# One visit to the quarters of the array: the block-diagonal product together with the next pair's k^T v and q^T

## The chip, the cores and the metric

The kernel runs on one core of one Trainium2 chip. Its time is the device time in microseconds (us) of one execution. Three executions of the kernel before took 942.20, 940.97 and 944.48 us, so the median is 942.2 us. The profiled execution has a span of 942.4 us and a granted TensorE clock of 1.000 throughout.

The engines are named as in the profile: PE is TensorE (matmuls; PEld its weight loads), DVE is VectorE, ACT is ScalarE, POOL is GpSimd and SP is SyncE, whose queue issues most of the transfers.

## The reference

There are two stages. The first is linear attention, on q, k and v of shape (8 batches, 8 heads, 576 rows, 64):

```
kv  = einsum('bhsd,bhse->bhde', k, v)
out = einsum('bhsd,bhde->bhse', q, kv)
rms = sqrt(mean(out * out, axis=-1) + 1e-06)
attn = out / rms * g_norm
```

Each head thus needs k^T v (64x64, a sum over 576 rows), the product of q with it, and a normalisation over the 64 columns of every row. The heads are laid side by side to x of 4608 x 512, and the second stage is a feed-forward block with w_in (512 x 2048) and w_out (2048 x 512):

```
h = x @ w_in
sp = maximum(h, 0) + log1p(exp(-abs(h)))
g = h * erf(sp)
return g @ w_out
```

## The kernel before

**Groups, pairs and tiles.** The rows are worked in nine groups T. Groups 0 to 7 are the first 512 rows (G) of each batch; group 8 is made of the 64 last rows (R) of all eight batches. A group's attention is done two heads at a time: four pairs p to a group (NP). A group's hidden layer is 16 tiles of 128 columns (FC), taken in four batches of four (BATCH), and then four projections j of 128 rows each.

**Three numbers for one.** From group 2 on (FIRST) the feed-forward matmuls don't use plain fp32. Each operand is cut into three fp32r forms, and `product` (L522) makes 12 matmuls of 128x512 for one 128x512 result: eight into n_ps and four into m_ps. `upper` (L478, ScalarE), `lower_only` (L481) and `both_only` (L484, VectorE) cut the forms: x_forms of the group's input and g_forms of the hidden layer. The weights' forms are written to DRAM in groups 0 and 1 and streamed back for each later group.

**The main loop** (L866) goes over rounds m, one for each batch b of each group. A round has four hidden tiles of the current batch, then the four projections of the batch before, and, in between, one pair of the *next* group's attention. So the attention of groups 3 to 7 is done in 20 rounds, while groups 2 to 6 go through their feed-forward block. In each round:

- hidden tile i: `product` on TensorE, then a scaled copy of n_ps on ScalarE (L916), an add of m_ps on VectorE (`add`, L518), and softplus on ScalarE (L931). In the first two tiles the g_forms of the batch before are cut as well (L478 twice on ScalarE, L481 and L484 twice on VectorE);
- after the fourth tile: erf over the batch (L935), behind a load of its function table;
- projection j: `result` (L840): `product`, then two VectorE operations into e (L513 or L851, and L518);
- after the second projection: the gating product h * s (L958).

**The pair's attention** is a list of pieces that `attention` (L282) returns, and `places` (L881) says where in the round each of them is put: (0, 2, 3, 5, 6, 8), where place 1 to 4 are after hidden tiles 1 to 4, and 5 to 8 after projections 1 to 4. In the last round of a group the sixth place is 7. The pieces for groups 1 to 7 are:

- `products` (L310), place 0, before the first hidden tile: k^T v for the two heads (ten matmuls of 115 or 116 rows and 64 columns, L326), and q^T by four 128x128 transposes (L353). For even pairs q_last, the last 64 rows of two pairs, is transposed as well (L334). VectorE copies k^T v to bd_kv (L340, then L342 twice, the two copies that swap partition halves), and the tail of q^T (L348); ScalarE copies q^T to qT (L354).
- `apply_quad` (L356), place 2: the block-diagonal product. The array is used as four quarters of 64x64; four matmuls of 256 columns (L362), and two for the tail (L370). The result stands in at_ps, a tile of two PSUM banks. ScalarE squares it (L374).
- `keep_tail` and `halve`, place 3: VectorE keeps the tail's result in x_last (L377) and cuts the square into two fp32r parts (L397, L398). `loads` then asks for the pair two rounds ahead.
- `mean`, place 5: four matmuls (L413, L414) that average over a head's columns, into the upper half of at_ps; then Ln, Exp and Square on ScalarE (L428, L429, L430), between two table loads.
- `norm`, place 6: three VectorE operations (L436, L439, L448), the last giving x.
- `split`, place 8: x to x_forms (L478, L481, L484).

**What sets the order.** The schedule is written by hand (`manual_schedule`): each engine runs its instructions in the order in which the program emits them. Within a round a piece's instructions therefore stand on ScalarE and VectorE behind those of the hidden tile just before its place, and ahead of those of the next. [...]two belong to at_ps, and six are handed out as three pairs by turns to `product` (the list `banks`, L520). A pair of banks comes free when the copy or add of both results is done.

**The layout of q.** For groups 1 to 7 each partition of q_sb holds four consecutive rows of q, and two of the four row blocks are loaded with the two heads swapped, by four transfers (L134 to L136). So the transposed q stands where the quarters want it. `store` (L600) writes the results back to rows in steps of four.

Of the kernel before, what the change touches and what calls it, by code (L numbers as in the profile page):

```python
# [39 lines left out]
FP32 = mybir.dt.float32  # L40
# [3 lines left out]
AF = mybir.ActivationFunctionType  # L44
# [10 lines left out]
FIRST = 2  # L55
# [5 lines left out]
def kernel(  # L61
# [56 lines left out]
    def chunks(T):  # L118

        return 6 if T == 0 else 5  # L120

    def load_pair(i):
        T, p = divmod(i, NP)
        if T >= B:
            return
        pool = early if i in (2, 3) else kvp
        side = nc.scalar if i < 3 else nc.sync
        t = q_sb[T, p] = pool.tile([P, J, 2, D], FP32, name="q_sb", tag="q")
        rows = q[T, 2 * p : 2 * p + 2, 0:G, :].rearrange("h (p j) d -> p j h d", j=J)
        if T == 0:  # L130
            nc.sync.dma_start(out=t, in_=rows)
        else:

            for i in range(2):  # L134
                for js, to in ((slice(0, J // 2), i), (slice(J // 2, J), 1 - i)):
                    nc.sync.dma_start(out=t[:, js, to], in_=rows[:, js, i])  # L136
        for name, got, src in (("k", k_sb, k), ("v", v_sb, v)):
            C = chunks(T)
            rows, rest = divmod(S, C)
            assert rest < 2  # L140
            t = got[T, p] = pool.tile([rows + rest, 2, C, D], FP32, name=f"{name}_sb", tag=name)
            heads = src[T, 2 * p : 2 * p + 2]
            side.dma_start(
                out=t[:rows].rearrange("r h c d -> r h (c d)"),
                in_=heads[:, : S - rest].rearrange("h (r c) d -> r h (c d)", c=C),
            )
            if rest:
                side.dma_start(
                    out=t[rows:, :, 0], in_=heads[:, S - rest :].rearrange("h r d -> r h d")
                )  # L150
# [125 lines left out]
    def at_pool(bufs):  # L276
# [2 lines left out]
        ps_now[:] = [at_room.enter_context(tc.tile_pool(name="ps_at", bufs=bufs, space=PSUM))]  # L279
        return ps_now[0]  # L280

    def attention(T, p, pools=None):  # L282

        st = {}

        halves = FIRST <= T < B
        quad = 0 < T < B
        side = (slice(0, D), slice(D, 2 * D))

        def two(t):  # L290
            return t.rearrange("p (a t) -> p a t", a=2) if quad else t
        bd = bd_kv[:, (T * NP + p) % 2, :]

        q_tail, o_tail = slice(P, 2 * P), slice(2 * P, 2 * P + R)

# [8 lines left out]
        def square_tile(name):  # L304

            if T == 0:
                return gate.tile([P, G], FP32, name=name, tag="h")
            return attp.tile([P, G], FP32, name=name, tag="qT")

        def products():  # L310

            if quad:

                pool = at_pool(2)
                kv_ps, qt_ps = (
                    pool.tile([P, G], FP32, name=name, tag="at") for name in ("kv_ps", "qt_ps")
                )
            else:
                kv_ps = st["kv"] = bank("kv_ps")
            ks, vs, qs = (x.pop((T, p)) for x in (k_sb, v_sb, q_sb))  # L320
            C = chunks(T)
            for c in range(C):
                rows = slice(0, S // C + (c < S % C))
                for i in range(2):
                    s = slice(i * D, i * D + D)
                    nc.tensor.matmul(  # L326
                        kv_ps[s, 0:D] if quad else kv_ps[s, s],
                        lhsT=ks[rows, i, c],
                        rhs=vs[rows, i, c],
                        start=(c == 0),  # L330
                        stop=(c == C - 1),
                    )
            if p % 2 == 0:
                nc.tensor.transpose(kv_ps[:, q_tail], q_last[:, p // 2], ident)  # L334
            if p == NP - 2:
                for i in range(NP):
                    load_last(T + 1, i)
            st["qT"] = square_tile("qT")
            if quad:
                nc.vector.tensor_copy(out=bd[:, 0:D], in_=kv_ps[:, 0:D])  # L340
                for i in range(2):
                    nc.vector.tensor_copy(out=bd[side[1 - i], D : 2 * D], in_=kv_ps[side[i], 0:D])  # L342
            else:
                for s in side:
                    nc.vector.tensor_copy(out=bd[s, s], in_=kv_ps[s, s])
            if p % 2 == 0:
                tails[T] = attp.tile([P, P], FP32, name="qT_last", tag="t")
                nc.vector.tensor_copy(out=tails[T], in_=kv_ps[:, q_tail])  # L348
            st["tail"] = tails[T][:, p % 2 * R : p % 2 * R + R]
            if not quad:  # L350
                qt_ps = bank("qt_ps")
            for j in range(J):
                nc.tensor.transpose(qt_ps[:, j * P : j * P + P], qs[:, j], ident)  # L353
            nc.scalar.copy(st["qT"], qt_ps)  # L354

        def apply_quad():  # L356

            qT, tail = st["qT"], st.pop("tail")
            at = st["at"] = at_pool(1).tile([P, 2, G], FP32, name="at_ps", tag="at")
            x = two(qT)  # L360
            for a, i, o in ((0, 0, 0), (0, 1, 1), (1, 0, 1), (1, 1, 0)):
                nc.tensor.matmul(  # L362
                    at[side[o], a, 0 : 2 * P],
                    lhsT=bd[side[i], a * D : a * D + D],
                    rhs=x[side[i], a],
                    start=True,
                    stop=True,
                )
            for s in side:
                nc.tensor.matmul(  # L370
                    at[s, 0, 2 * P : 2 * P + R], lhsT=bd[s, 0:D], rhs=tail[s], start=True, stop=True
                )
            st["o"] = at[:, :, 0 : 2 * P]
            nc.scalar.activation(x, st["o"], AF.Square)  # L374

        def keep_tail():
            nc.vector.tensor_copy(  # L377
                out=x_last[:, p, T * R : T * R + R], in_=st["at"][:, 0, 2 * P : 2 * P + R]
            )

        def apply():
            qT, o_ps, kv_ps = st["qT"], bank("se_ps"), st.pop("kv")
            nc.tensor.matmul(kv_ps[:, o_tail], lhsT=bd, rhs=st.pop("tail"), start=True, stop=True)
            nc.tensor.matmul(o_ps, lhsT=bd, rhs=qT, start=True, stop=True)
            nc.vector.tensor_copy(out=x_last[:, p, T * R : T * R + R], in_=kv_ps[:, o_tail])
            st["o"] = o_ps
            nc.scalar.activation(qT, o_ps, AF.Square)

        def square():
            st["o"], st["qT"] = x_last[:, p, :], square_tile("sq")  # L390
            nc.scalar.activation(st["qT"], st["o"], AF.Square)

        def halve():
            sq = st.pop("qT")
            hi = st["hi"] = attp.tile([P, G], FP32R, name="sq_hi", tag="rms_r")
            lo = st["lo"] = attp.tile([P, G], FP32R, name="sq_lo", tag="sq_lo")
            nc.vector.tensor_copy(out=hi, in_=sq)  # L397
            nc.vector.tensor_tensor(out=lo, in0=sq, in1=hi.bitcast(FP32), op=ALU.subtract)  # L398

        def mean(table=True):  # L400
# [13 lines left out]
                    nc.tensor.matmul(ps, lhsT=mean_w, rhs=lo[:, a], start=False, stop=True)  # L414
                u = square_tile("u")
            else:
                u = st.pop("qT")
                for ps, a in parts:
                    nc.tensor.matmul(
                        ps, lhsT=mean_w.bitcast(FP32), rhs=two(u)[:, a], start=True, stop=True  # L420
# [38 lines left out]
                thirds(st.pop("x"), *(form[:, p] for form in x_forms[T]))  # L459

        def loads():
            load_pair(T * NP + p + 2)

        if T == 0:
            return products, apply, halve, mean, norm
        if T == B:
            return lambda: None, square, lambda: None, mean, norm, split

        if halves:
            pieces = ((products,), (apply_quad,), (keep_tail, halve, loads))  # L470
        else:
            pieces = ((products, loads), (apply_quad,), (keep_tail,))
        return (*(partial(chain, *group) for group in pieces), mean, norm, split)


# [43 lines left out]

    banks = [(ps_h, "h"), (ps_h, "h")] + [(ps_o, f"o{i}") for i in range(4)]  # L520

    def product(weights, moving, turns=True, cuts=1):  # L522


        n_ps, m_ps = (
            pool.tile([P, G], FP32, name=name, tag=tag)
            for name, (pool, tag) in zip(("n_ps", "m_ps"), banks[:2])
        )
        if turns:
            banks.extend(banks[:2])  # L530
            del banks[:2]
        spans = [slice(i * G // cuts, (i + 1) * G // cuts) for i in range(cuts)]
        for ps, forms, cols in [(n_ps, (0, 1), slice(0, G))] + [(m_ps, (2,), x) for x in spans]:
            for k in range(4):
# [64 lines left out]

    def store(T, j, e, cols=slice(0, DM)):  # L600
        if T < B:
            rows = out[T * S : T * S + G, :].rearrange("(p j) f -> p j f", j=J)
            nc.sync.dma_start(out=rows[:, j, :], in_=e)
            return
        for h, side in enumerate((nc.sync, nc.scalar)):
            first_row = (2 * j + h) * S + G
            side.dma_start(
                out=out[first_row : first_row + R, cols], in_=e[h * R : h * R + R, cols]
            )
# [388 lines left out]
```

## Time and profile before

| | share or time |
|---|---|
| span of the profiled execution | 942.4 us |
| TensorE busy | 923.0 us, 98% |
| VectorE busy | 721.1 us, 77% |
| ScalarE busy | 617.3 us, 66% |
| chain that ended last: TensorE, VectorE, ScalarE | 48%, 22%, 19% |
| mean DMA rate | 276 GB/s |
| k^T v, L326: 656 records | 27.8 us, 235 ns each |
| q^T, L353: 128 records | 21.0 us, 289 ns each |
| block-diagonal product, L362: 224 records | 18.6 us, 402 ns each |
| its tail, L370: 112 records | 7.9 us, 217 ns each |
| k^T v to bd_kv, L340 and L342 | 6.1 us and 12.4 us |
| q^T to SBUF, L354 | 18.7 us |

One plain fp32 matmul shows as two records in the trace. Matmuls overlap in the array, so the mean duration of a record is longer than the time from one start to the next, and the latter is what counts in a stream. "Busy" of a matmul engine in a dense stream is near 100% whatever it does. Durations of VectorE and ScalarE instructions are also somewhat longer than the distance between the starts of two that follow each other (the 128x512 copy L916 takes 0.59 us, and the next can start 0.47 us after a PSUM read of that size began).

The rounds of groups 3 to 7's attention lie between about 254 and 748 us; the rows below in the prediction are from there.

### The profile page before, as it was taken

How to read it: one execution, taken by the hardware profiler on the slowest of the kernel's cores; microseconds unless marked ns; L12 is line 12 of the kernel's file. 1: busy time of each engine (PE TensorE's matmuls, PEld its weight loads, DVE VectorE, ACT ScalarE, POOL GpSimd, SP SyncE). 2: the span in 40 equal slices, each digit the busy share in tenths (PEclk: the TensorE clock that was granted, in tenths of full speed). 3: DMA queues.
4: the chain of work that ended last, by engine and by line, in shares of the span. 5: the costliest groups of instructions: out<-in, count | busy, mean ns of one | idle time of the engine just before them, and what ended most of it. 6: DMA issues, size and time to landing. Idle time of an engine off the chain costs nothing.

```text
span 942.4 us, 12548 instructions
## 1 busy us (share of the span) xinstructions
PE 923.0 (98%) x4556; PEld 683.0 (72%) x4556; DVE 721.1 (77%) x1046; ACT 617.3 (66%) x825; POOL 2.4 (0%) x10
## 2 busy tenths in 40 slices
PE   5899999999999999999999999999999999999998
PEld 4444445566588888888888888888888788888886
DVE  2857648888578888888888888888888877788667
ACT  3899776778666666666666666666666666665552
POOL 1000000000000000000000000000000000000000
PEclk9999999999999999999999999999999999999999
DMA  9776405888699888898889889988896779777972
GB/s 252 253 213 213 145 19 197 328 337 338 209 360 352 316 311 282 301 330 290 275 297 328 293 280 328 319 297 287 290 337 250 265 251 355 274 279 290 354 272 60
DMA packets 109605, 259.83 MB, mean 276 GB/s; under 512 B 45336, under 2 KB 68200, under 8 KB 109544
## 3 DMA queue, kind: packets, MB, share of 16 engines
q1 hardware_dynamic: 107832, 256.74, 77.4%
q10 hardware_dynamic: 1648, 2.29, 0.9%
q8 instruction: 36, 0.59, 0.2%
q14 instruction: 25, 0.20, 0.1%
q0 software_dynamic: 64, 0.00, 0.0%
HBM read 224.40 MB, written 34.60 MB: 275 GB/s over the span
## 4 chain that ended last, share of the span: by engine, by line
PE 48%; DVE 22%; ACT 19%; issue 6%; DMA 4%; SPq 1%; DVEq 0%; ACTq 0%
PE n_ps L536 21%; PE m_ps L536 10%; PE o_ps L592 9%; DVE h L518 5%; PE h_ps L766 4%; DVE g_forms L481 4%; ACT s L935 4%; DVE e L518 2%; ACT L105 2%; ACT s L931 2%; ACT L935 2%; ACT h L916 2%; DMA q_sb<-in_q_dram 2%; DVE e L513 2%; DVE x L448 1%
## 5 line engine op out<-in xcount | busy, mean ns | idle before, releaser
L536 PE MATMUL n_ps<-w_out_parts,g_forms 128*128 128x512 f32 x928 | 232.0, 392 | 0.0
L536 PE MATMUL n_ps<-x_forms,w_in_parts 128*128 128x512 f32 x896 | 226.8, 395 | 0.3 <-DVE x_forms L481 0.3
L536 PEld LDWEIGHTS n_ps<-w_out_parts,g_forms 128*128 128x128 f32 x928 | 172.8, 188 | 37.1 <-issue 1.4
L931 ACT ACTIVATE s<-h 128x512 f32<-128x512 f32 x112 | 70.9, 633 | 184.7 <-DVE h L518 184.7
L536 PEld LDWEIGHTS n_ps<-x_forms,w_in_parts 128*128 128x128 f32 x896 | 165.2, 188 | 35.1 <-DVE x_forms L481 0.8
L518 DVE TENSOR_TENSOR h<-m_ps,h 128x512 f32<-128x512 f32 x116 | 79.8, 688 | 59.5 <-ACT h L916 44.8
L536 PE MATMUL m_ps<-w_out_parts,g_forms 128*128 128x512 f32 (+1 forms) x468 | 124.2, 388 | 0.0
L536 PE MATMUL m_ps<-x_forms,w_in_parts 128*128 128x512 f32 x448 | 120.1, 390 | 0.0
L592 PE MATMUL o_ps<-w_out_sb,h_sb 128*128 128x512 f32 x224 | 101.5, 596 | 0.2 <-DVE h_sb L716 0.2
L536 PEld LDWEIGHTS m_ps<-w_out_parts,g_forms 128*128 128x128 f32 x468 | 87.5, 188 | 18.5
L536 PEld LDWEIGHTS m_ps<-x_forms,w_in_parts 128*128 128x128 f32 x448 | 84.1, 188 | 18.1
L518 DVE TENSOR_TENSOR e<-m_ps,e 128x512 f32<-128x512 f32 (+1 forms) x117 | 80.3, 687 | 18.3 <-PE m_ps L536 11.5
L513 DVE SCALAR_TENSOR_TENSOR e<-n_ps,e 128x512 f32<-128x512 f32 x88 | 60.3, 686 | 33.4 <-PE n_ps L536 32.3
L592 PEld LDWEIGHTS o_ps<-w_out_sb,h_sb 128*128 128x128 f32 x224 | 41.4, 190 | 44.4 <-issue 41.9
L484 DVE SCALAR_TENSOR_TENSOR g_forms<-g_forms 128x1024 fp32r<-128x1024 f32 x58 | 71.1, 1225 | 2.0
L481 DVE TENSOR_TENSOR g_forms<-h,g_forms 128x1024 fp32r<-128x1024 f32 x58 | 70.4, 1215 | 1.2 <-ACT g_forms L478 1.2
L766 PE MATMUL h_ps<-xT,w_in_sb 128*128 128x512 f32 x144 | 64.6, 594 | 3.4 <-DVE w_in_sb L245 1.9
L916 ACT ACTIVATE h<-n_ps 128x512 f32<-128x512 f32 x112 | 65.6, 586 | 3.1 <-PE n_ps L536 3.0
L478 ACT ACTIVATE g_forms<-h 128x1024 fp32r<-128x1024 f32 x58 | 58.9, 1058 | 12.2 <-PE m_ps L536 8.7
L958 DVE TENSOR_TENSOR h<-h,s 128x1024 f32<-128x1024 f32 x56 | 66.0, 1219 | 0.7 <-ACT s L935 0.7
L108 ACT ACT_TABLE_LOAD x44 | 56.5, 1283 | 0.7
L935 ACT ACTIVATE s<-s 128x1024 f32<-128x1024 f32 x56 | 56.2, 1052 | 0.3
(108 smaller groups left out, 990.8 us busy)
## 6 DMA issues: line engine op xcount, KB each, us to landing
w_out_parts<-w_out SPq DMA_DIRECT2D x116, 768.0 KB
w_in_parts<-w_in SPq DMA_DIRECT2D x112, 768.0 KB
w_in<-w_new SPq DMA_DIRECT2D x16, 768.0 KB
w_raw<-in_moe_w_in_dram SPq DMA_DIRECT2D x16, 512.0 KB
w_raw<-in_moe_w_out_dram SPq DMA_DIRECT2D x8, 1024.0 KB
out_dram<-e SPq DMA_DIRECT2D x32, 256.0 KB
k_sb<-in_k_dram SPq DMA_DIRECT2D x28, 287.5 KB
v_sb<-in_v_dram SPq DMA_DIRECT2D x28, 287.5 KB
```

Of the source, the lines that this page charges most:

```text
L478: nc.scalar.activation(high, x, AF.Copy, scale=1.0 + 2.0**-13)
L481: nc.vector.tensor_tensor(out=low, in0=x, in1=high.bitcast(FP32), op=ALU.subtract)
L484: nc.vector.scalar_tensor_tensor(out=both, in0=low.bitcast(FP32), scalar=SHIFT, in1=high.bitcast(FP32), op0=ALU.mult, op1=ALU.add,)
L513: nc.vector.scalar_tensor_tensor(out=out_, in0=ps, scalar=scale, in1=out_, op0=ALU.mult, op1=ALU.add)
L518: nc.vector.tensor_tensor(out=out_, in0=ps, in1=out_, op=ALU.add)
L536: nc.tensor.matmul(ps[:, cols], lhsT=weights(form, k), rhs=moving(form, k)[:, cols], start=(form == forms[0] and k == 0), stop=(form == fo ...
L592: nc.tensor.matmul(o_ps[j], lhsT=g[:, j * P : j * P + P], rhs=w_out_sb[:, f, :], start=(f == 0), stop=last,)
L766: nc.tensor.matmul(plain[i], lhsT=w_in_sb[:, i % FC, c], rhs=xT[T][:, c, :], start=(c == 0), stop=(c == KC - 1),)
L916: nc.scalar.activation(h[:, i], n_ps, AF.Copy, scale=SHIFT - 1.0)
L931: nc.scalar.activation(s[:, i], h[:, i], AF.Softplus)
L935: nc.scalar.activation(part(s, i), part(s, i), AF.Erf)
L958: nc.vector.tensor_tensor(out=part(h, half), in0=part(h, half), in1=part(s, half), op=ALU.mult)
```

## The change

The change has one aim: TensorE should change between its whole array, its column halves and its quarters less often.

- k^T v and q^T are written so that they use the four quarters too. `kv_products` splits each chunk of k and v rows into 64 rows and the rest (51 or 52): 20 matmuls in place of 10, whose two row halves go to two different PSUM banks and are added afterwards. `turn_products` makes q^T from 16 matmuls of 64x64 with the identity in place of four transposes (and four for q_last in place of one). These write every fourth column of their bank, so that qT is in the order of q's rows.
- From group 3 on, `visit` takes the place of `apply_quad`: after the six matmuls of this pair's block-diagonal product it issues the *next* pair's q^T and k^T v, four and four by turns. k^T v goes to free columns of at_ps, q^T to a pair of banks from the list `banks`. The pieces at place 0 are then empty, except for the first pair of group 3, which is prepared by itself (`prepare`), as are all pairs of groups 1 and 2.
- The copies follow: `turned` makes two ScalarE copies of 128x256 out of the two banks, after the Square; `kv_kept` has VectorE add the two banks' halves of k^T v (a reduce, `tensor_reduce`) and make the two copies that swap partition halves, now from SBUF, after `halve` and the tail's copy.
- q is loaded for all groups by one transfer in one order, and `store` writes blocks of 128 consecutive rows. Loads are asked for one pair earlier in the count, since a pair's tiles are now used one round earlier.

The diff, cut to its core:

```diff
-        rows = q[T, 2 * p : 2 * p + 2, 0:G, :].rearrange("h (p j) d -> p j h d", j=J)
-        if T == 0:
-            nc.sync.dma_start(out=t, in_=rows)
-        else:
-            for i in range(2):
-                for js, to in ((slice(0, J // 2), i), (slice(J // 2, J), 1 - i)):
-                    nc.sync.dma_start(out=t[:, js, to], in_=rows[:, js, i])
+        nc.sync.dma_start(
+            out=t, in_=q[T, 2 * p : 2 * p + 2, 0:G, :].rearrange("h (p j) d -> p j h d", j=J)
+        )
...
+    def turn_products(T, p, ps):
+        qs = q_sb.pop((T, p))
+        for j in range(J):
+            for r in range(2):
+                for i in range(2):
+                    out_ = ps[r][rows_of[i if r == 0 else 1 - i], 0 : 2 * P]
+                    yield partial(
+                        nc.tensor.matmul,
+                        out_.rearrange("d (t j) -> d j t", j=J)[:, j],
+                        lhsT=qs[rows_of[r], j, i],
+                        rhs=ident[rows_of[r], rows_of[r]],
...
+    def kv_products(T, p, at, crossed):
+        ks, vs = (x.pop((T, p)) for x in (k_sb, v_sb))
+        C = chunks(T)
+        for c in range(C):
+            for r in range(2):
+                rows = (slice(0, D), slice(D, S // C + (c < S % C)))[r]
+                for i in range(2):
+                    yield partial(
+                        nc.tensor.matmul,
+                        at[rows_of[i], r ^ i if crossed else r, kv_cols],
+                        lhsT=ks[rows, i, c],
+                        rhs=vs[rows, i, c],
+                        start=(c == 0),
+                        stop=(c == C - 1),
+                    )
+
+    def turned(T, p, ps):
+        qT = attp.tile([P, G], FP32, name="qT", tag="qT")
+        if isinstance(ps, tuple):
+            for a in range(2):
+                nc.scalar.copy(halves_of(qT)[:, a], ps[a][:, 0 : 2 * P])
+        else:
+            nc.scalar.copy(halves_of(qT), ps[:, :, 0 : 2 * P])
+        if p % 2 == 0:
+            tails[T] = attp.tile([P, 2, R], FP32, name="qT_last", tag="t")
+            for a in range(2):
+                t = ps[a] if isinstance(ps, tuple) else ps[:, a]
+                nc.vector.tensor_copy(out=tails[T][:, a], in_=t[:, 2 * P : 2 * P + R])
...
+    def kv_kept(T, p, at):
+        kv = kv_of(T, p)
+        nc.vector.tensor_reduce(
+            out=kv[:, 0:D],
+            in_=at[:, :, kv_cols].rearrange("p a e -> p e a"),
+            op=ALU.add,
+            axis=mybir.AxisListType.X,
+        )
+        for i in range(2):
+            nc.vector.tensor_copy(out=kv[rows_of[1 - i], D : 2 * D], in_=kv[rows_of[i], 0:D])
...
+            st["next"] = fused and then[0] < B
+            if st["next"]:
+                ps = pair_of_banks("q0_ps", "q1_ps")
+                kvs = list(kv_products(*then, at, crossed=True))
+                turns = list(turn_products(*then, ps))
+                while kvs or turns:
+                    for some in (turns, kvs):
+                        for product_ in some[:4]:
+                            product_()
+                        del some[:4]
...
-            nc.scalar.activation(x, st["o"], AF.Square)
+            nc.scalar.activation(two(st["sq"]), st["o"], AF.Square)
+            if st["next"]:
+                turned(*then, ps)
...
         def keep_tail():
...
+            if st["next"]:
+                kv_kept(*then, st["at"])
...
-            pieces = ((products,), (apply_quad,), (keep_tail, halve, loads))
+            pieces = ((prepare_,), (visit,), (halve, keep_tail, loads))
+        if fused:
+            first_ = (prepare_,) if (T, p) == (FIRST + 1, 0) else ()
+            pieces = (first_, (visit,), (halve, keep_tail, loads))
...
-            rows = out[T * S : T * S + G, :].rearrange("(p j) f -> p j f", j=J)
-            nc.sync.dma_start(out=rows[:, j, :], in_=e)
+                rows = rows.rearrange("(j p) f -> j p f", j=J)
+            nc.sync.dma_start(out=rows[j], in_=e)
```

## The prediction

> **What bounds the kernel now.** I read the page's busy times first.
>
> ```profile
> PE 923.0 (98%) x4556; PEld 683.0 (72%) x4556; DVE 721.1 (77%) x1046; ACT 617.3 (66%) x825; POOL 2.4 (0%) x10
> ```
>
> TensorE looks like the only limit. So I asked who waited for whom while groups 3 to 7 are prepared (300 to 745 us). No wait of TensorE's matmuls is listed, but two lines set VectorE and ScalarE against each other:
>
> ```profile
> ACT s L931 <- DVE h L518: 121.8, 72, 3.4
> DVE h L518 <- ACT h L916: 28.4, 17, 1.7
> ```
>
> The columns are total us, times, longest. These two engines wait for each other, not for TensorE. Then I read VectorE's and ScalarE's timelines over one round (one pair, one batch of four feed-forward tiles): start, duration, instruction, idle time before.
>
> ```profile
> 530.29 0.22 DVE L340 COPY bd_kv<-kv_ps 128x64 f32<-128x64 f32 x1
> 530.52 0.46 DVE L342 COPY bd_kv<-kv_ps 64x64 f32<-64x64 f32 x2
> 530.90 1.21 DVE L481 TENSOR_TENSOR g_forms<-h,g_forms 128x1024 fp32r<-128x1024 f32 x1
> ...
> 536.40 0.68 DVE L518 TENSOR_TENSOR h<-m_ps,h 128x512 f32<-128x512 f32 x1
> 538.76 0.69 DVE L518 TENSOR_TENSOR h<-m_ps,h 128x512 f32<-128x512 f32 x1 [1.67 <-ACT h L916]
> 539.36 0.21 DVE L377 COPY x_last<-at_ps 128x64 f32<-128x64 f32 x1
> 539.50 0.42 DVE L397 CAST sq_hi<-qT 128x512 fp32r<-128x512 f32 x1
> 539.95 0.69 DVE L398 TENSOR_TENSOR sq_lo<-qT,sq_hi 128x512 fp32r<-128x512 f32 x1
> 540.63 0.69 DVE L518 TENSOR_TENSOR h<-m_ps,h 128x512 f32<-128x512 f32 x1
> ...
> 548.68 0.69 DVE L436 SCALAR_TENSOR_TENSOR u<-at_ps,u 128x512 f32<-128x512 f32 x1
> ```
>
> ```profile
> 537.12 0.63 ACT L931 ACTIVATE s<-h 128x512 f32<-128x512 f32 x1 [1.87 <-DVE h L518]
> 537.66 0.58 ACT L374 ACTIVATE qT<-at_ps 128x512 f32<-128x512 f32 x1
> 538.13 0.59 ACT L916 ACTIVATE h<-n_ps 128x512 f32<-128x512 f32 x1
> 539.48 0.63 ACT L931 ACTIVATE s<-h 128x512 f32<-128x512 f32 x1 [0.76 <-DVE h L518]
> ...
> 548.02 0.63 ACT L430 ACTIVATE u<-rms_r 128x512 f32<-128x512 f32 x1
> ```
>
> Read as one chain, this closes on itself: L436 of one round, the other two norm steps, e and x_forms, L340 and L342, L481/L484 twice, h of the second tile (536.40), softplus (537.12), Square (537.66), copy (538.13), third tile's h (538.76), fourth tile's h (540.63), softplus, erf, three norm steps of ScalarE, L436 again at 548.68, 0.03 us after L430 ends. No step waits for TensorE. In every round of 326 to 746 us L436 starts 0.03 us after L430's end, and the rounds take 24.80 and 24.62 us in turn (the longer has L348's tail copy), mean 24.71. TensorE's own round is as long, with no gap: 96 matmuls of 0.227 us are 21.77, k^T v with the transposes 1.43, the block-diagonal product 0.89, the means 0.48, and 0.13 of uneven pace after each of the three insertions. So two limits lie on top of each other.
>
> At the last group boundary the chain is seen to hold TensorE:
>
> ```profile
> 750.63 0.50 PE L536 MATMUL n_ps<-x_forms,w_in_parts 128*128 128x512 f32 x1 [0.33 <-DVE x_forms L481]
> ```
>
> A group's first hidden tile needs the last pair's x_forms. There it follows the last projection with no k^T v between. At the earlier boundaries that 1.43 us insertion was the cushion.
>
> **What the Trainium skill says.** "TensorEngine Tiling (Array Packing)", Key Properties: a change of tiling mode drains TensorE, and tiles load and multiply in parallel. The trace agrees with both: 96 matmuls run without a gap, yet each insertion costs 0.3 to 0.4 us beyond its matmuls, and the eight 64x256 records of L362, 0.40 us each, take 0.66 us together. "PSUM — Partial Sum Buffer", Engine vs sequencer instructions: ScalarE and VectorE queues are strict FIFO; the chain above shows it. "ScalarE: Activation LUTs", What happens when an `exp` ACTIVATE runs: 0.833 ns an element; the trace gives (1058 - 633)/512 = 0.83.
>
> **The change, TensorE.** Per pair it removes the insertion of 1.43 us. In it k^T v takes 20 records, each column half starting one every 58 ns: 0.58 us. Four transposes at 0.11 are 0.44. The remaining 0.4 us is three mode changes. It adds to the visit 16 q^T and 20 k^T v matmuls, two records each: 72, spread evenly over the four quarters, 18 per quarter. At 58 ns each that is 1.04 us, plus 0.12 for tails every other pair, 1.10 on average. So the gain is the mode changes: 1.45 - 1.10 = 0.35 us, 24.71 to about 24.35 us a round. The trace has no run of 64-column matmuls on four quarters. Low end: the 58 ns just used. High end: 29 ns a record (two halves, as now), 2.2 us, which would make 25.5. The skill ("TensorE: Matmul & The Clock Gate", Wait — 56ns, not 53.3ns?) gives about 25 ns as the least distance between starts, but L362's four starts lie 7 ns apart on different quarters, so I take the low end.
>
> **The change, the chain.** Removed from its start: L340 and L342, 530.29 to 530.90, 0.61 us (0.18 more in alternate rounds for L348), so the chain without them and without tails is 24.62 - 0.61 = 24.01 us. The old qT copy (L354) was off the chain: ScalarE waits 0.9 us for the transposes before it.
>
> Added on ScalarE: qT now comes as two 128x256 copies between Square and the third tile's copy L916, which is next in its queue and which VectorE's third h awaits. A 512-wide Square here occupies 0.47 us start to start; 256 elements less is 0.21 less, so 0.26 each, 0.52 together. Bounds: 0.47 (elements alone) and 0.75 (a full fixed cost each).
>
> Added on VectorE: the reduce over two banks and two 64x64 copies, queued before the fourth tile's h. In 538.76 to 540.63 both ways to the fourth h take 1.87 us (VectorE's queue, and softplus plus copy on ScalarE), so nothing hides them. The reduce reads 128 elements, as the 128x128 PSUM copy does: 0.29 us. The first copy waits for its end. Both cross partition halves like L342, which repeats every 0.19. Sum 0.29 + 0.02 + 0.38 = 0.69; bounds 0.49 (copies at the memset's 0.11, partly overlapped) and 0.80.
>
> New chain: 24.01 + 0.52 + 0.69 = 25.22 us, with bounds 24.97 and 25.56. It exceeds TensorE's 24.35, so it sets the round. The tails' two copies fit in VectorE's 1.67 us of idle before the third h. TensorE will run ahead until a group boundary, then stand until x_forms arrives.
>
> **Beside or free.** One q load in place of four, and stores by contiguous 128-row blocks: DMA's busy share is 0.87 in this stretch, but matmuls wait for no load; nothing. The prefetch distance stays two rounds. Q^T takes one bank pair more per round, so tiles 3 and 4 reuse pairs after one tile and a visit (4.7 us) instead of 6.3: the first tile's h ends 6.6 us after that tile begins, tile 3's m_ps starts 9.3 after; hidden. Mean now waits for the reduce, ready before the first projection's end: hidden. Groups 1 and 2 and the first pair of 3 use the quartered products in a visit of their own: one mode change less against 1.04 to 1.16 for 1.02 to 1.18, nothing to 0.1 us a pair, 0.3 in all.
>
> **Sum.** First round (before the chain has closed; VectorE's e waits for TensorE): visit longer by 1.10, +1.1. Next 18: 18 x 25.22 = 454.0. The last, with no next pair: 24.0. Together 478.0 against 469.4 now (L436 from 276.96 to 746.38): +8.6. With +1.1 and +0.3: 942.2 + 10.0, about 952.
>
> **Rivals.** (1) TensorE bounds and the chain yields: 19 x 0.35 saved, 942.2 - 6.7 = 935.5. For it: 98% busy and no gaps. Against: at best 0.47 + 0.49 is added to the chain and 0.70 on average removed. (2) The chain grows by the least, 24.97 us: 18 x 0.25 less, 947.5; with small overlaps besides, 945. For it: bounds are from rows of other shapes. (3) Quarters don't run four at a time: 25.5 us a round, 19 x 0.8 + 0.3, 957.5. For it: no row shows it. Against: L362's overlap.
>
> **Chances.** Forecast 0.62 (949 to 955), rival 2 0.18, rival 3 0.10, rival 1 0.10. Half of rival 2 falls within 0.5%, so faster 0.09, same 0.11, slower 0.80. The range runs from 944.5 to 958: it leaves out rival 1 and the far ends.
>
> **What would show it.** L436's successors should start about 25.2 us apart, 0.03 us after ScalarE's last norm step; the two 256-wide copies should occupy 0.5 us and reduce plus copies 0.7 us; VectorE's third h should still wait for ScalarE; a visit should be near 2.0 us; TensorE should gain idle time or long matmul gaps at the first hidden tile of each group, 2 to 3 us. Wrong if rounds are below 24.7 us, if those new pieces show idle engines around them, or if a visit takes 3 us.

## The result and the profile after

The changed kernel takes 954.75 us (median of 4), the kernel before, on the same chip, 943.18: a ratio of 1.0126, with a 95% interval of 1.0100 to 1.0152. It is slower, by 1.3%. The profiled spans are 952.8 and 942.4 us.

In the code below L628 is the add of h and e (L518 before), L1034 the copy of n_ps (L916), L1049 softplus (L931), L472 the visit's Square (L374), L338 the copies of q^T, L354 and L361 the reduce and the two copies of k^T v, L539 the first norm step (L436) and L533 ScalarE's last (L430). L650 is `product` (L536).

First the page's busy times for the changed kernel (engine, busy us, share of the span, instructions):

```profile
PE 924.1 (97%) x5998; PEld 685.8 (72%) x5998; DVE 720.2 (76%) x1060; ACT 617.2 (65%) x844; POOL 2.4 (0%) x10
```

Against 923.0, 683.0, 721.1 and 617.3 us no engine's busy time has grown by more than 2.8 us (the weight loads'), while the span has grown by 10.4 us. The time is in waits and order. The waits of the changed kernel from 300 to 745 us (who waits, for whom; us in total, times, longest) show where:

```profile
ACT s L1049 <- DVE h L628: 142.0, 69, 4.1
...
DVE u L539 <- ACT u L533: 18.2, 15, 1.9
DVE h L628 <- ACT h L1034: 17.7, 15, 2.2
...
PEld n_ps L650 <- ACT x_forms L588: 5.1, 4, 1.4
PEld n_ps L650 <- DVE x_forms L591: 4.6, 4, 1.1
PE n_ps L650 <- ACT x_forms L588: 3.4, 4, 1.0
PE n_ps L650 <- DVE x_forms L591: 3.3, 4, 0.8
```

The line of L539 is the telling one: VectorE now sits idle for ScalarE's last norm step in 15 of 18 rounds, 18.2 us in all. The kernel before, in the same window, had

```profile
DVE e L513 <- PE n_ps L536: 23.2, 16, 1.6
...
DVE u L436 <- ACT u L430: 1.3, 8, 0.2
```

And TensorE, which had no such line before, stands (sits idle) for x_forms, four times, once at each group boundary in the window.

Next one round of the changed kernel. VectorE, by start (us), duration, instruction, and idle time before it:

```profile
505.74 0.69 DVE L539 SCALAR_TENSOR_TENSOR u<-at_ps,u 128x512 f32<-128x512 f32 x1 [0.61 <-ACT u L533]
...
511.97 1.22 DVE L591 TENSOR_TENSOR g_forms<-h,g_forms 128x1024 fp32r<-128x1024 f32 x1
...
517.36 0.68 DVE L628 TENSOR_TENSOR h<-m_ps,h 128x512 f32<-128x512 f32 x1
520.26 0.69 DVE L628 TENSOR_TENSOR h<-m_ps,h 128x512 f32<-128x512 f32 x1 [2.22 <-ACT h L1034]
520.87 0.42 DVE L500 CAST sq_hi<-sq 128x512 fp32r<-128x512 f32 x1
521.32 0.69 DVE L501 TENSOR_TENSOR sq_lo<-sq,sq_hi 128x512 fp32r<-128x512 f32 x1
521.93 0.21 DVE L477 COPY x_last<-at_ps 128x64 f32<-128x64 f32 x1
522.06 0.28 DVE L354 TENSOR_REDUCE bd_kv<-at_ps 128x64 f32<-128x128 f32 x1
522.37 0.39 DVE L361 COPY bd_kv<-bd_kv 64x64 f32<-64x64 f32 x2
522.80 0.69 DVE L628 TENSOR_TENSOR h<-m_ps,h 128x512 f32<-128x512 f32 x1
...
530.84 0.69 DVE L539 SCALAR_TENSOR_TENSOR u<-at_ps,u 128x512 f32<-128x512 f32 x1 [1.45 <-ACT u L533]
```

ScalarE in the same round:

```profile
518.07 0.63 ACT L1049 ACTIVATE s<-h 128x512 f32<-128x512 f32 x1 [1.88 <-DVE h L628]
518.61 0.58 ACT L472 ACTIVATE sq<-at_ps 128x512 f32<-128x512 f32 x1
519.09 0.64 ACT L338 COPY qT<-q_ps 128x256 f32<-128x256 f32 x2
519.60 0.62 ACT L1034 ACTIVATE h<-n_ps 128x512 f32<-128x512 f32 x1
...
530.18 0.63 ACT L533 ACTIVATE u<-rms_r 128x512 f32<-128x512 f32 x1
```

The two copies of q^T hold the third tile's copy from 519.09 to 519.60, and VectorE's third h, idle for 2.22 us, starts at 520.26. The reduce and the copies of k^T v stand from 522.06 ahead of the fourth h at 522.80. From third to fourth h it was 1.87 us (538.76 to 540.63), now 2.54. L539 starts 0.03 us after L533 ends (530.81). In this trace 15 of the 18 rounds from 277.92 to 732.88 us, those that prepare a next pair, take 25.10 us, each closed with the same 0.03; before, the mean was 24.71. For comparison, the round of the kernel before whose lines stand in the prediction opens with

```profile
524.06 0.69 DVE L436 SCALAR_TENSOR_TENSOR u<-at_ps,u 128x512 f32<-128x512 f32 x1 [0.15 <-ACT u L430]
```

TensorE runs ahead and stands at a group's first hidden tile, here at group 4's (PE, same columns):

```profile
453.81 1.07 PE L650 MATMUL m_ps<-w_out_parts,g_forms 128*128 128x512 f32 x4
454.71 1.52 PE L650 MATMUL n_ps<-x_forms,w_in_parts 128*128 128x512 f32 x6
457.22 0.49 PE L650 MATMUL n_ps<-x_forms,w_in_parts 128*128 128x512 f32 x1 [0.99 <-ACT x_forms L588]
458.55 0.51 PE L650 MATMUL n_ps<-x_forms,w_in_parts 128*128 128x512 f32 x1 [0.84 <-DVE x_forms L591]
458.89 1.21 PE L650 MATMUL m_ps<-x_forms,w_in_parts 128*128 128x512 f32 x4
459.90 3.51 PE L650 MATMUL n_ps<-x_forms,w_in_parts 128*128 128x512 f32 x8
```

The sixth matmul of the second line starts at 455.85 us (five times the pace of 0.227 after 454.71). From it to the next it is 1.37 us, and then 1.33: 2.25 us lost here, 1.75 to 2.25 at the four boundaries. The last line is told of at the end.

### The profile page after: what moved, and what is told of

It is laid out like the page before. It is cut to its first block, busy times and chain, and to the rows that moved or that the text cites. A ratio compares the mean times of both kernels' runs of the same rounds, so it can differ in the third digit from the quotient of the medians.

```text
span 952.8 us, 15391 instructions
## 1 busy us (share of the span) xinstructions
PE 924.1 (97%) x5998; PEld 685.8 (72%) x5998; DVE 720.2 (76%) x1060; ACT 617.2 (65%) x844; POOL 2.4 (0%) x10
## 4 chain that ended last, share of the span: by engine, by line
PE 65%; DVE 15%; ACT 11%; DMA 4%; issue 3%; SPq 0%; DVEq 0%; ACTq 0%
PE n_ps L650 31%; PE m_ps L650 16%; PE o_ps L706 9%; PE h_ps L884 4%; DVE h L628 3%; ACT s L1053 2%; DVE g_forms L591 2%; DVE e L628 2%; DMA w_raw<-in_moe_w_in_dram 1%; ACT L105 1%; ACT L1053 1%; DMA w_in_parts<-w_in 1%; PE at_ps L446 1%; DVE x L551 1%; DVE u L542 1%
## 5 line engine op out<-in xcount | busy, mean ns | idle before, releaser
L650 PE MATMUL n_ps<-x_forms,w_in_parts 128*128 128x512 f32 x896 | 229.8, 397 | 9.0 <-DVE x_forms L591 4.2
L650 PE MATMUL n_ps<-w_out_parts,g_forms 128*128 128x512 f32 x928 | 232.5, 392 | 0.9 <-DVE qT_last L345 0.9
L1049 ACT ACTIVATE s<-h 128x512 f32<-128x512 f32 x112 | 70.8, 633 | 209.7 <-DVE h L628 209.7
L650 PEld LDWEIGHTS n_ps<-x_forms,w_in_parts 128*128 128x128 f32 x896 | 168.2, 190 | 49.1 <-ACT x_forms L588 6.0
L650 PEld LDWEIGHTS n_ps<-w_out_parts,g_forms 128*128 128x128 f32 x928 | 172.5, 188 | 39.3 <-DVE qT_last L345 2.2
L650 PE MATMUL m_ps<-w_out_parts,g_forms 128*128 128x512 f32 (+1 forms) x468 | 124.3, 388 | 0.0
L650 PE MATMUL m_ps<-x_forms,w_in_parts 128*128 128x512 f32 x448 | 120.8, 392 | 0.0
L628 DVE TENSOR_TENSOR h<-m_ps,h 128x512 f32<-128x512 f32 x116 | 79.7, 687 | 52.4 <-ACT h L1034 34.9
L650 PEld LDWEIGHTS m_ps<-w_out_parts,g_forms 128*128 128x128 f32 x468 | 87.5, 188 | 18.4
L650 PEld LDWEIGHTS m_ps<-x_forms,w_in_parts 128*128 128x128 f32 x448 | 84.5, 189 | 17.8
L628 DVE TENSOR_TENSOR e<-m_ps,e 128x512 f32<-128x512 f32 (+1 forms) x117 | 80.3, 687 | 16.7 <-PE m_ps L650 8.4
L1034 ACT ACTIVATE h<-n_ps 128x512 f32<-128x512 f32 x112 | 66.0, 590 | 4.5 <-PE n_ps L650 4.4
```

The source lines that it names most:

```text
L628: nc.vector.tensor_tensor(out=out_, in0=ps, in1=out_, op=ALU.add)
L650: nc.tensor.matmul(ps[:, cols], lhsT=weights(form, k), rhs=moving(form, k)[:, cols], start=(form == forms[0] and k == 0), stop=(form == fo ...
L1034: nc.scalar.activation(h[:, i], n_ps, AF.Copy, scale=SHIFT - 1.0)
L1049: nc.scalar.activation(s[:, i], h[:, i], AF.Softplus)
```

## The experiments

My theory: the closed chain of VectorE and ScalarE sets the round at 25.10 us, and what lengthened it are the two pieces above, 0.51 and 0.67 us. The rivals: the products on the quarters (TensorE), or a transfer, set it. The ratios below are to the kernel before on the same chip, with 95% intervals. A "round" is the distance between first norm steps in the trace.

**Each piece off the chain by its order alone.** First, the reduce and the copies of k^T v queued in VectorE's idle time ahead of the third h:

```diff
 # visit()
             if st["next"]:
+                kv_kept(*then, at)
                 turned(*then, ps)
 # keep_tail()
-            if st["next"]:
-                kv_kept(*then, st["at"])
```

> The next pair's reduce and two 64x64 copies are queued on VectorE ahead of the third tile's h (in its 2.2 us of idle time) instead of ahead of the fourth's; nothing else is changed. Chain theory (VectorE and ScalarE's closed chain sets the round at 25.10 us): the 0.67 us leave the chain, 24.43 us a round, 18 x 0.67 = 12.1 less than 954.8, about 942.7 us, and down to 940 if the waits at the group boundaries shrink too. Rival (TensorE's products on the quarters, or a transfer, set the round): no change, 953 to 956.

Measured: 941.91 us, 0.9996 (0.9985 to 1.0007). Rounds 24.44 us, one in four, at a group boundary, 24.70; the mean is 24.50.

Second, the copies of q^T (and the visit's matmuls in program order, which doesn't move them on TensorE) ahead of the second tile's softplus; Square becomes a piece of its own and stays:

```diff
-        places = (0, 2, 3, 5, 6, 8)
+        places = (0, 1.5, 2, 3, 5, 6, 8)
...
 # the hidden tile
                     evacuate()
+                pieces(i + 0.5)
                 nc.scalar.activation(s[:, i], h[:, i], AF.Softplus)
 # visit(), pieces
-            nc.scalar.activation(two(st["sq"]), st["o"], AF.Square)
...
-            pieces = (first_, (visit,), (halve, keep_tail, loads))
+            pieces = (first_, (visit,), (square_,), (halve, keep_tail, loads))
```

> The two 128x256 copies of q^T are queued on ScalarE ahead of the second tile's softplus (in 1.9 us of its idle time) instead of between Square and the third tile's copy; Square stays where it is. Chain theory: 0.51 us leave the chain, 24.59 us a round, 18 x 0.51 = 9.2 less, about 945.6 us (943 if the boundary waits shrink). Rival (TensorE or a transfer sets the round): no change, 953 to 956.

Measured: 943.73 us, 1.0012 (1.0004 to 1.0021). Rounds 24.56 us, one in four 24.70, mean 24.59. Its second round, before these, takes 28.49 us; the section on the start comes back to it.

Third, both of these edits:

> Both moves at once. Chain theory: the chain is 25.10 - 0.51 - 0.67 = 23.92 us and falls below TensorE's own work of about 24.35 us a round, which then binds: 18 x 0.75 = 13.5 less and the 2.5 us of the two long boundary rounds, 938 to 941 us, faster than both kernels. If TensorE had no such bound, 18 x 1.18 = 21 less, 933.5. Rival (nothing of this is on the path): no change, 953 to 956.

Measured: 940.95 us, 0.9980 (0.9971 to 0.9988). Rounds 24.26, 24.40, 24.71 and 24.40 by turns, mean 24.44.

Fourth, the opposite sign, with `for a in (0, 1, 0, 1)` in place of `range(2)` around the copies of q^T:

> The two 128x256 copies of q^T are made twice, in place, on ScalarE; nothing else is changed. Chain theory: 0.51 us more in the chain, 25.61 us a round, 18 x 0.51 = 9.2 more, about 964 us. Rival (TensorE or a transfer sets the round and ScalarE has room): no change, 953 to 956.

Measured: 963.28 us, 1.0214 (1.0198 to 1.0230). Rounds 25.65 us, but for two of 26.3 at group boundaries. ScalarE's queue in that kernel:

```profile
549.77 0.58 ACT L472 ACTIVATE sq<-at_ps 128x512 f32<-128x512 f32 x1
550.25 1.19 ACT L338 COPY qT<-q_ps 128x256 f32<-128x256 f32 x4
551.29 0.64 ACT L1034 ACTIVATE h<-n_ps 128x512 f32<-128x512 f32 x1
```

Four copies hold the third tile's copy for 1.04 us instead of 0.51, and the round is 0.55 longer. What follows from the four: away from the boundaries each piece costs its own length in a round (0.66 and 0.54 us less when moved, 0.55 more when doubled), although it costs nothing in the same engine's idle time a few instructions earlier. With both moved the mean gain is 0.66 a round, not 1.20: another limit is met. The reduce alone already comes near it (0.60 on the mean). In the kernel with both early, VectorE shows which:

```profile
510.63 0.68 DVE L631 TENSOR_TENSOR h<-m_ps,h 128x512 f32<-128x512 f32 x1
511.23 0.28 DVE L354 TENSOR_REDUCE bd_kv<-at_ps 128x64 f32<-128x128 f32 x1
511.55 0.39 DVE L361 COPY bd_kv<-bd_kv 64x64 f32<-64x64 f32 x2
512.99 0.69 DVE L631 TENSOR_TENSOR h<-m_ps,h 128x512 f32<-128x512 f32 x1 [1.05 <-ACT h L1037]
...
519.48 0.69 DVE L626 SCALAR_TENSOR_TENSOR e<-n_ps,e 128x512 f32<-128x512 f32 x1 [1.64 <-PE n_ps L653]
520.40 0.69 DVE L631 TENSOR_TENSOR e<-m_ps,e 128x512 f32<-128x512 f32 x1 [0.23 <-PE m_ps L653]
521.01 2.35 DVE L1080 TENSOR_TENSOR h<-h,s 128x1024 f32<-128x1024 f32 x2
523.28 0.68 DVE L542 SCALAR_TENSOR_TENSOR u<-at_ps,u 128x512 f32<-128x512 f32 x1
```

The reduce lies in a gap of which 1.05 us are still idle. The norm (L542) now waits for nothing of ScalarE's; it follows the gate, which follows two projections that VectorE had to wait for TensorE to make (1.64 and 0.23 us).

**Is TensorE's work on the path?** In the changed kernel, four fifths of k^T v left out of the shared visit:

```diff
-        for c in range(C):
+        used = 1 if crossed else C
+        for c in range(used):
...
-                        stop=(c == C - 1),
+                        stop=(c == used - 1),
```

> The changed kernel with only the first of the five chunks of k^T v in the shared visit; the other 16 of its 36 extra matmuls (and the sum they make) are left out, so TensorE has 8 records a quarter less, 8 x 58 ns = 0.46 us a round. Chain theory: rounds stay at 25.10 us and the time at 953 to 956 us; TensorE only stands longer at the group boundaries. Rival (the work on the quarters sets the round): 18 x 0.46 = 8.3 less, about 946.5 us.

Measured: 954.87 us, 1.0139 (1.0123 to 1.0154). The visit becomes 0.47 us shorter (1.50 us and 1.63 with tails, where it was 1.97 and 2.10), and the rounds stay at 25.10, but for two of 25.85 at group boundaries. Then the same edit on top of both early moves:

> Both moves as in the run with both early, and only the first of the five chunks of k^T v in the shared visit; the rest of that sum is left out. TensorE has 0.46 us less a round, 24.44 - 0.46 = 23.98, just above the chain's 23.92. If TensorE binds once both moves are made: 18 x 0.46 = 8.3 less than 940.95, about 932.5 us. If the chain bound there as in the changed kernel: no change, 940 to 942.

Measured: 934.91 us, 0.9913 (0.9900 to 0.9926). Rounds of 23.88, 23.90, 24.22 and 23.93 by turns, mean 23.98; the second round, told of below, takes 27.90 us, 2 more than with both early, and the time is 2.4 us over the expectation. The same 0.47 us on TensorE are worth nothing under the chain and all of themselves once the chain is out of the way.

**Did two limits coincide before?** Three kernels, all from the kernel before. (Where expectations here and below name group 4, the code begins with group 3.) Square ahead of the second tile's softplus (the visit as a whole at place 1.5, with the added `pieces(i + 0.5)` as above):

> The kernel before, with the block-diagonal visit's Square queued on ScalarE ahead of the second tile's softplus, in its idle time; TensorE's order is as it was. Its VectorE/ScalarE chain gets 0.48 us shorter, 24.23 us. Two coinciding limits: TensorE's 24.71 us a round still binds, no change, 942 to 944 us. If the chain alone bound the kernel before: 19 x 0.48 = 9.1 less, 934. If TensorE alone bound it: no change.

```diff
 # products()
-            C = chunks(T)
+            C = chunks(T) if T <= FIRST else 1
...
```

> The kernel before, with only the first of the five chunks of k^T v from group 4 on; the rest of that sum is left out. TensorE has 16 records less at 29 ns, 0.46 us a round, 24.25. Two coinciding limits: the chain's 24.71 us still binds, no change, 942 to 944 us. If TensorE alone bound the kernel before: 19 x 0.46 = 8.8 less, 934. If the chain alone bound it: no change.

> The kernel before with both edits (Square ahead of the second tile's softplus; four fifths of the sum k^T v left out from group 4 on). Two coinciding limits: both are now near 24.25 us a round, and only here the time falls, by 19 x 0.46 = 8.7, to about 934 to 936 us. If neither were on the path (a transfer or a fixed schedule sets the round): no change, 942 to 944.

Measured:

| kernel | us | ratio, interval | rounds |
|---|---|---|---|
| Square early | 941.53 | 0.9984 (0.9975 to 0.9992) | 24.58 and 24.72 |
| fewer products | 941.87 | 0.9998 (0.9990 to 1.0006) | 24.61 and 24.80 |
| both | 932.91 | 0.9906 (0.9892 to 0.9919) | 24.12 and 24.31 |

942.82 us is the kernel before here: by the medians 1.3 and 0.9 us alone (the interval of the second includes no change), 9.9 together: that is what two coinciding limits look like. The 1.3 us were not expected; they agree with a round of 24.65 us on the mean in place of 24.71, so TensorE's limit lay some 0.06 us under the chain's. The waits from 300 to 740 us name the limit that is left. With Square early VectorE waits more for the projections (23.2 us before), and no wait of the norm for ScalarE is listed:

```profile
DVE e L513 <- PE n_ps L536: 31.6, 27, 1.6
```

With fewer products the norm waits for ScalarE in all 18 rounds, and TensorE stands longer ahead of k^T v (the weight loads 15.2 us, 6.9 before); for this wait the trace names no engine:

```profile
PEld kv_ps L326 <- issue: 15.2, 18, 0.9
DVE u L436 <- ACT u L430: 10.6, 18, 0.6
PE kv_ps L326 <- issue: 8.1, 18, 0.5
```

**The start.** In the changed kernel's trace the second round takes 25.81 us, 24.61 before. TensorE waits there, near 291 us, as the kernel before doesn't (waits of 250 to 300 us):

```profile
PE n_ps L650 <- DMA w_in_parts<-w_in: 0.9, 1, 0.9
```

The first round with a shared visit loads two pairs, since pairs are now asked for three rounds ahead. Put the second of these loads at the end of its round:

```diff
 # loads()
-            if fused:
+            if fused and (T, p) != (FIRST + 1, 0):
                 load_pair(T * NP + p + 3)
 # split()
+            if (T, p) == (FIRST + 1, 0):
+                load_pair(T * NP + p + 3)
```

> Both moves as in the run with both early, and in the first round of group 4's attention, which loads two pairs, the second pair's loads are queued at the end of the round, behind its weight loads. If those loads hold up the weights that a hidden tile waits for near 291 us: 1.2 us less than with both early (940.95), about 939.7 us, and the second round shrinks from 25.87 to about 24.6 us. If the wait there has another cause: no change, 940 to 942.

> As the run with the late load, and Square is queued ahead of the second tile's softplus too, so that the whole visit's VectorE and ScalarE work lies in idle time. The chain falls by another 0.48 us to 23.45 us. If TensorE binds at 24.4 us a round: no change from the late load's run but the 0.3 us stands at the group boundaries, 938 to 940 us. If the chain still had a part in it: up to 18 x 0.4 = 7 less, 932.

Measured: 943.21 us, 1.0001 (0.9992 to 1.0009), and 942.29, 0.9996 (0.9988 to 1.0004). A miss for both: the second round is 24.40 as hoped, but the third takes 27.57 (27.37 with Square early). The later rounds are those of the kernel with both early, 24.26, 24.40 and 24.70, so with Square moved as well the chain has no part left in them. The waits of 250 to 330 us in the second of these kernels:

```profile
PE n_ps L651 <- DMA w_in_parts<-w_in: 2.8, 2, 1.6
```

The wait moved one round on and grew. In the first of the two kernels the same two waits (1.4 and 1.6 us) are put down to ScalarE's instructions, so that they are loads there too is inferred. It seems not to be the place but the extra pair itself. The last kernel has no extra pair; it loads two rounds ahead, and has the whole visit early:

```diff
-            if not fused or (T, p) == (FIRST + 1, 0):
-                load_pair(T * NP + p + 2)
-            if fused:
-                load_pair(T * NP + p + 3)
+            load_pair(T * NP + p + 2)
```

> The whole visit's VectorE and ScalarE work in idle time (as in the run with visit early and late load), and each round of groups 4 to 7 loads the pair two ahead instead of three, so that no round loads two pairs and a pair's loads have about 20 us instead of 44 before their products. If the extra pair's loads hold up weights near the start (1.2 us with both early, 3 us with the late load): the second and third rounds are 24.4 us, about 937 to 939.5 us. If 20 us are too short for the loads: visits wait for q, k or v and rounds are over 24.7 us, 945 or more. If the start's wait has another cause: 940 to 942.

Measured: 938.84 us, 0.9953 (0.9939 to 0.9966), with rounds of 24.40 and 24.26 at the start and a mean of 24.44. No wait of TensorE for a load is listed. So the extra pair was the cause. It is the fastest full kernel of this study, 4.7 us under the kernel before on its chip; the changed one was 11.6 over it on another.

The same extra pair costs very unequal amounts: the second round takes 25.81 us in the changed kernel, but 28.49 with the copies early and 27.90 in the kernel with both early and fewer products. In these two the stand for the load is 1.9 and 2.1 us, and the eight matmuls behind it take 3.44 and 3.21 us in place of 1.98, at a granted clock near 0.6. That slow stretch is the subject of the last section.

## Why the prediction was right, point by point

- **Which limit sets the round: right, and shown.** The chain binds (25.10 us against TensorE's 24.33 away from the boundaries); moving either piece, doubling one, and taking work from TensorE answer as the chain says. The rivals "TensorE bounds" and "quarters don't run four at a time" are out: less TensorE work changed nothing, and the visit took 1.97 us, 2.10 with tails, mean 2.03, where 2.0 was said (what it adds between the matmuls on its two sides at their pace of 0.227). This agrees with the Trainium skill, "TensorEngine Tiling (Array Packing)", Key Properties (tiles multiply in parallel): 18 records a quarter, 1.10 us more than the visit of 0.93 before. One reading of the waits was too strong: "not for TensorE" left out the line of 23.2 us above, VectorE's waits for projections. They end before the norm's own last wait, which is ScalarE's by 0.03 us; they show how close TensorE's limit lay.
- **The chain's terms.** ScalarE's copies: 0.52 foreseen, 0.51 measured. (The 0.833 ns an element behind it stands in the Trainium skill, "ScalarE: Activation LUTs", under Step-by-step: what each stage is for; the trace gave 0.83.) Reduce and copies: 0.69 foreseen, 0.67 measured (from third to fourth h). Removed at the start: 0.61 foreseen; from the norm to the first g_forms it went from 6.84 us to 6.23, so 0.61 (524.06 to 530.90 before, 505.74 to 511.97 after). Another 0.11 us went between the g_forms and the second h (530.90 to 536.40 became 511.97 to 517.36), which I hadn't foreseen and whose cause no run separates. That is most of the difference between 25.10 and 25.22 us.
- **TensorE's gain: near, by a sum that doesn't add up.** With the chain out of the way TensorE's rounds are 24.58 and 24.72 us in the kernel before (Square early), and 24.26 and 24.40 with both early (away from the boundaries): 0.32 a round, where 0.35 was foreseen. The removed insertion, listed as 1.43 and summed as 1.45, takes 1.36 us and 1.47 with tails, mean 1.42. But the parts given for TensorE's round, with 0.13 after each of three insertions, add up to 24.96 us and not 24.71. Measured with the uneven pace inside each insertion they are 21.77, 1.42, 0.93 and 0.52, so 24.64, and the round is 24.65. TensorE had a little slack in the kernel before.
- **"Matmuls wait for no load": wrong once.** I priced the prefetch distance at nothing, but getting one pair further ahead means one round with two pairs' loads. It cost the second round about 0.7 us beyond 25.10.
- **TensorE's stand at the boundaries: right in place and near in size** (1.75 to 2.25 us, said 2 to 3), but I took it as free. Twice it was not: two rounds took 26.33 us each, 2.5 beyond 25.10 together. The last section shows what they have in common.
- **The sum.** First round: +1.1 foreseen, +1.15 measured (245.31 to 277.92, was 245.50 to 276.96). Rounds from there to the last norm: 478.0 foreseen, 478.84 measured (277.92 to 756.76). The chain was 0.12 x 18 = 2.2 us shorter than said, while the boundaries' 2.5 and the start's 0.7 came on top; that these errors cancel is luck. Groups 1 and 2: +0.3 foreseen, -0.2 measured. In all 10.0 us were foreseen; the spans differ by 10.4 and the medians by 11.6.
- **Tails and the bank pair:** the tails' copies are hidden, since rounds with and without them are both 25.10. The turn of the banks isn't quite free: three times TensorE's weight loads waited for the tails' copy (L345) to give a pair back, 0.9 us at most, and twice its matmuls, 0.9 us together. No round grew by it.

## What to carry to other kernels

When a fused step saves time on the engine that looks busiest, price its evacuation on the other engines first, and ask into which queue position it falls: the same three VectorE instructions cost 0.67 us a round ahead of one add and nothing ahead of the add before it. Where two limits coincide, relieving either shows next to nothing, so test them in pairs before calling an edit worthless. A longer prefetch distance has a price of its own in the round in which it is built up.

## What the runs showed of the hardware

After two of the four stands TensorE ran at about half its pace. The windows of the changed kernel after the stand shown above (stretch: its us, busy us and count of PE, PEld, DVE, ACT, POOL, the granted clock, DMA share, GB/s):

```profile
455.00:459.50 4.50, 2.68 (x11) 1.68 (x10) 4.29 (x7) 3.50 (x5) 0.00 (x0) 1.00 0.53 175
459.50:463.30 3.80, 3.80 (x12) 2.96 (x11) 3.66 (x5) 0.20 (x1) 0.00 (x0) 0.55 0.46 171
463.30:468.00 4.70, 4.70 (x98) 3.71 (x97) 3.27 (x4) 2.48 (x6) 0.00 (x0) 1.00 0.59 189
```

Eight matmuls start 427 ns apart in place of 227, some 1.5 us lost, and the round that follows is one of 26.33 us; the same happens at 661 us. In both the norm no longer follows ScalarE but the gate, behind projections that VectorE waited for (1.05 and 1.65 us in the first of them). At 356 and 557 us TensorE stood 1.75 and 2.2 us, no slow stretch follows, and the rounds are 25.10. Other runs show the same pairing. The two rounds of 26.3 us with the copies made twice, the two of 25.85 with fewer products, and the long second rounds told of above each hold one such stretch, in which windows of 1 us show a granted clock of 0.50; their other boundary rounds hold none.

The Trainium skill, "TensorE: Matmul & The Clock Gate", What's actually happening, has a clock that halves after an idle window of about 3.4 us, in windows that run freely. The halving and the length of the slow stretch agree with this trace. The idle time was shorter here: two stands of 1.1 us with one matmul between were enough, sometimes, and at the start a single one of 1.9 us. What decides it was not tried. With both pieces moved TensorE loses 0.40 us at a boundary, and no such stretch follows.

A pair's loads are long in the issuing. SyncE's queue in the changed kernel, at the second of the two pairs (start, us, transfer):

```profile
270.62 0.66 SPq L129 DMA_DIRECT2D q_sb<-in_q_dram  x1
271.38 1.76 SPq L138 DMA_DIRECT2D k_sb<-in_k_dram  x1
273.19 2.35 SPq L143 DMA_DIRECT2D k_sb<-in_k_dram  x1
...
276.67 0.40 SPq L787 DMA_DIRECT2D w_out_parts<-w_out  x1
277.17 0.38 SPq L787 DMA_DIRECT2D w_in_parts<-w_in  x1
```

The two pairs together keep the queue from 262.0 to 276.6 us, and the weights behind them go out only then. Around that time (274.75 to 277.00 us) the DMA engines are 0.36 busy at 109 GB/s, against 1.01 at 416 GB/s from 259 to 268 us. So just there the weights waited for the queue that issues them rather than for a full DMA; why these issues take so long was not tried. From 284 to 290 us, just ahead of TensorE's stand, the DMA engines are full again (1.00 to 1.06, 415 to 430 GB/s). Which part of the late load is due to the queue and which to the full DMA is therefore not shown.
